# Attention and MLP kernel: batch 0 turned by float32 products on TensorE instead of DMA transposes, first matrix loaded in 4 KB rows

## Chip, core and metric

The kernel runs on one core of a Trainium2 chip. The metric is device time in microseconds (us) of one execution. The core has TensorE (PE, matrix products into PSUM), VectorE (DVE), ScalarE (ACT), GpSimd (POOL) and SyncE (SP), each with its own instruction queue that runs in order, and 16 DMA engines. SP's queue issues most transfers; ACT's queue issues the loads of the two weight matrices.

## The reference

Attention with a local window of 32 positions and 32 global tokens, over 8 batches and 8 heads, and behind it a two-layer MLP on the rows of the result:

```python
s_g = scale * q_g @ k_all.T;  out_g = sm(s_g) @ v_all          # 32 global rows
s_ll = where(abs(i - j) <= 32, scale * q_l @ k_l.T, -1e9)      # 512 local rows
s_l = concat([scale * q_l @ k_g.T, s_ll])
out_l = sm(s_l) @ concat([v_g, v_l])
x = concat([out_g, out_l]) as [8*544, 512]
h = x @ w_in                                                   # [512, 2048]
g = h * tanh(softplus(h))
return g @ w_out                                               # [2048, 512]
```

The two matrices arrive as 64-bit floats.

## The kernel before

**Numbers in two parts.** Products that must be exact run on pairs of float16 numbers: each operand is scaled by a power of two and split into a high part (rounded) and a low part (the remainder), and a product is three float16 products (high-high, high-low, low-high). This is done for probabilities (P to ph), for V (vraw to vf), for attention's result (x to xs), for both matrices (W) and for the MLP's middle (e to G).

**Attention.** A unit is (batch, pair of heads, quarter of 128 rows); there are 16 in a batch. `scores` makes two score tiles s (float32 products); `row_max` adds the mask and takes the row extreme into P on DVE; `expo` makes exponentials on ACT; `p_hi` and `p_lo` split P into ph; `p_turn` turns ph by a DMA transpose of 256 KB into pt, since the next product needs probabilities with the key along the partitions; `pv` multiplies pt with the moved parts of V (va, vc) into U. After two quarters (four, from batch 2 on) `x_norm`, `x_split` and `x_turn` divide, split and turn the result into xh and xl by two more DMA transposes. Global rows go the same way (g, gP, gph, gpt, gu).

**V.** `v_hi` and `v_lo` split, `v_move` places pieces by small SBUF to SBUF transfers.

**Weights.** Each matrix comes in 16 pieces of 512 KB (`w_load`, k below 16 is the first matrix w1). `w_bits` (L401) and `w_sum` (L408, L410) make 32-bit floats out of the 64-bit words, three DVE instructions a piece. `w_stat` sums squares on TensorE (tile ws, L421), `w_norm` (L428) reduces them to a scale once all 16 pieces are there, and only then `w_split` makes high and low parts of the eight column groups. The low part is either a DVE instruction (L471) or, for the groups in `BY_PE`, a product on TensorE: the scaled float32 original by a diagonal matrix dg (L465) minus the high part (L466) into a PSUM tile rest, copied by ACT or DVE. `BY_PE` holds the odd groups of both matrices.

**MLP.** The 4352 rows are 17 blocks of 256. `m1_mm` (L766, tile h) makes a step of the first layer, `mish` (L809) and `g_hi`, `g_lo` (L822) the activation and its parts, `m2_mm` (L834, tile o) the second layer, `store` the output.

**PSUM.** Ring h has two tiles (for the first layer, and for rest of the first matrix), o two, sc three for scores, u one.

**The order** is made by class `Plan` while the program is built: each task has an engine (or a choice of two), an estimated time, its dependencies and a priority; `order` simulates the engines by these estimates and emits each engine's list. Priorities follow `slot(u)`, which is called for each unit and the steps of blocks that `BLOCKS`, `PACE` and `LAGX` put beside it; `BOOST` is added to the MLP's tasks. Loads and conversions of the weights get slots from `LOAD1`, `CONV1`, `CONV2`, `FIRST1`, `FIRST2` and their steps. The estimate of a DMA transpose is `kib * 8` ns.

Of the kernel before, what the change touches and what calls it, by code (L numbers as in the profile page):

```python
# [49 lines left out]
class Plan:  # L50
# [10 lines left out]
    DEEP, SHARE, ISSUE = 3, 1.25, 450  # L61

    def __init__(self):
        self.tasks = []
# [24 lines left out]

    def add(self, eng, ns, fn, r=(), w=(), new=(), pri=0, rows=1.0, table=None):  # L90
# [41 lines left out]
        self.tasks.append((eng if isinstance(eng, list) else [(eng, ns)], fn, deps, after, new, n + pri + self.late if self.slot is None else -1e6 + self.slot * self.PER, rows, table))  # L132

    def order(self):
# [11 lines left out]
        moved, far = 0, []  # L146
# [40 lines left out]
        for _ in range(N):  # L187
            t, pri, e, n, ns = min(c for c in map(first, free) if c)
            start[n], on[n] = t, e
            if self.tasks[n][7] == "dma":  # L190
                far.append((max(t + self.DMA_IN, far[-1]) if far else t + self.DMA_IN) + ns * self.SHARE)
# [16 lines left out]
            if e == DMA:  # L208
                moved = max(moved, t) + ns
# [23 lines left out]
def attn_mish_kernel(ctx: ExitStack, tc: tile.TileContext, qt, kt, vm, vg, qg, w1, w2, consts_in, out, w64):  # L233
# [22 lines left out]
    def rings(pool, *table):  # L256
        for tag, bufs, shape, dt in table:
# [13 lines left out]
          ("wm", 2, [128, 1], F32), ("dg", 1, [128, 128], F32), ("pg", 1, [128, 2], F32), ("c", 3, [128, 3], F32),  # L271
# [102 lines left out]
    def words(k):  # L374
        return raw(k).rearrange("p (f w) -> p f w", w=2)

    def w_load(k):
        j, hf = HV[k]

        def go():  # L380
            n = 2 if w64 else 1
            dst = raw(k) if w64 else wf(k).bitcast(I32)
            if j < 8:
                nc.scalar.dma_start(dst.rearrange("p (c f) -> p c f", c=2),
                     w1[hf * 256:(hf + 1) * 256, j * 256 * n:(j + 1) * 256 * n].rearrange("(c p) f -> p c f", p=128))
# [6 lines left out]
        else:  # L392
            pl.add(ACT, dma(256), go, w=[wkey(j, hf)], table="dma")
# [3 lines left out]
    def w_bits(k):  # L397
        if not w64:
            return
        f, key = lambda: wf(k).bitcast(I32), wkey(*HV[k])  # L400
        pl.add(DVE, 360, lambda: V.tensor_scalar(f(), words(k)[:, :, 1], 3, 0x3FFFFFFF, ALU.logical_shift_left, ALU.bitwise_and),  # L401
               r=[rawkey(k)], w=[key])

    def w_sum(k):
        if not w64:
            return
        f, key = lambda: wf(k).bitcast(I32), wkey(*HV[k])
        pl.add(DVE, 610, lambda: V.scalar_tensor_tensor(f(), words(k)[:, :, 1], -0x40000000, f(), ALU.bitwise_and, ALU.bitwise_or),  # L408
               r=[rawkey(k)], w=[key])
        pl.add(DVE, 610, lambda: V.scalar_tensor_tensor(f(), words(k)[:, :, 0], 29, f(), ALU.logical_shift_right, ALU.bitwise_or),  # L410
               r=[rawkey(k)], w=[key])

    def w_stat(k):
# [3 lines left out]
        def go():  # L417
            u = wf(k).bitcast(BF16).rearrange("p (c two) -> p c two", two=2)
            for c in range(4):
                a = u[:, c * 128:(c + 1) * 128, 1]  # L420
                T.matmul(X["ws", w][:, :128], a, a, start=(k % 16 == 0 and c == 0), stop=(k % 16 == 15 and c == 3))  # L421
        pl.add(PE, mm(4, 131), go, r=[wkey(*HV[k])], w=[("ws", w)] if k % 16 else (),
# [51 lines left out]
    BY_PE = (1, 3, 5, 7, 9, 11, 13, 15)  # L474
# [632 lines left out]
```

## Time and profile before

| | us |
|---|---|
| runs | 1015.36, 1017.23, 1020.26; median 1017.23 |
| profiled execution, its own time | 1018.66 |
| its span, first to last instruction | 1016.9 |
| TensorE busy | 930.3 |
| ScalarE busy | 622.5 |
| VectorE busy | 566.0 |
| mean granted clock of TensorE | 0.991 |

Lines name L-number, engine, operation, and output tile<-input tiles. In rows of groups, busy time and mean ns of one stand after the first bar, idle time ahead of them and its releaser after the second. In rows of waits, the waiter stands left of the arrow; total us, times and longest follow. In rows of the timeline, start and length come first, and idle time before stands in brackets. In the lines of tenths a digit is the busy share in one of 40 equal slices. "SPq" and "ACTq" are the queues' issuing instructions. The product of two float32 operands shows as two MATMUL records, so "x2" at L465 is one product. PE's records overlap; from start to start is what one costs.

### The profile page before, as it was taken

Reading aid. Unit: us, or ns where it says so; the run is one execution under the profiler, and the core shown is the slowest. Engines: PE = TensorE matmul, PEld = TensorE weight load, DVE = VectorE, ACT = ScalarE, POOL = GpSimd, SP = SyncE. Lnnn points to the kernel's source line nnn. Section 1 sums busy time; section 2 is a strip of 40 time slices with the busy share of each in tenths; the row PEclk is TensorE's granted clock in tenths of the full one; section 3 lists DMA queues with packets and bytes.
Section 4 is the critical chain, followed back from the end, with each engine's and each line's share of the span. In section 5 each row is a group of like instructions: output and inputs, shape, how many; then the busy total and the mean of one; then the engine's idle time right before and its main releaser. Section 6 shows DMA issues by size and latency. Waiting matters only on the chain.

```text
span 1016.9 us, 20471 instructions
## 1 busy us (share of the span) xinstructions
PE 930.3 (91%) x7952; PEld 614.5 (60%) x7952; DVE 566.0 (56%) x1738; ACT 622.5 (61%) x1216; POOL 11.9 (1%) x22
## 2 busy tenths in 40 slices
PE   3245879999999899999999999999999999999996
PEld 2123555666656566666666666666666666666663
DVE  5468985657677655565556555655555554322221
ACT  2215586667667688689867986788688673211110
POOL 2000000000000000000000000000000000000000
PEclk9999989999999999999999999999999999999998
DMA  9996554747696975475446545644453432000000
GB/s 344 235 252 154 159 109 96 152 94 167 141 180 145 183 147 114 109 154 121 101 106 159 104 98 103 163 106 105 102 123 62 82 61 61 21 1 22 1 22 21
DMA packets 237946, 118.98 MB, mean 117 GB/s; under 512 B 202649, under 2 KB 216089, under 8 KB 236825
## 3 DMA queue, kind: packets, MB, share of 16 engines
q1 hardware_dynamic: 231192, 100.90, 46.1%
q10 hardware_dynamic: 6656, 16.78, 5.2%
q8 instruction: 62, 1.02, 0.4%
q14 instruction: 36, 0.29, 0.1%
HBM read 46.32 MB, written 8.91 MB: 54 GB/s over the span
## 4 chain that ended last, share of the span: by engine, by line
PE 78%; DMA 10%; DVE 6%; ACT 3%; SPq 2%; issue 1%; POOL 0%; ACTq 0%
PE o L834 32%; PE h L766 32%; PE s L579 5%; PE U L630 4%; DMA pt<-ph 3%; DMA vc<-vf 2%; PE g L668 2%; PE gu L722 1%; SPq L313 1%; DMA vraw<-in_vm 1%; DMA q<-in_qt 1%; DMA wraw<-in_w 1%; DVE W L410 1%; DVE W L408 1%; ACT P L594 1%
## 5 line engine op out<-in xcount | busy, mean ns | idle before, releaser
L834 PE MATMUL o<-W,G 128*128 128x512 f16 x1632 | 389.6, 380 | 1.8 <-DVE vmx L500 1.2
L766 PE MATMUL h<-xh,W 128*128 128x256 f16 x2048 | 378.6, 274 | 4.2 <-ACT e L809 4.2
L766 PEld LDWEIGHTS <-W 128*128 128x128 f16 x3264 | 309.0, 98 | 75.6 <-issue 15.9
L766 PE MATMUL h<-xl,W 128*128 128x256 f16 x1024 | 279.8, 273 | 0.0
L834 PEld LDWEIGHTS <-G 128*128 128x128 f16 x1632 | 156.7, 98 | 152.8 <-issue 5.7
L809 ACT ACTIVATE e<-h,c 128x512 f32<-128x512 f32 (+1 forms) x137 | 93.4, 684 | 150.8 <-PE h L766 144.0
L594 ACT ACTIVATE P<-P,nm 128x192 f32<-128x192 f32 (+1 forms) x256 | 118.0, 461 | 77.0 <-DVE nm L585 47.0
L326 DVE TENSOR_SCALAR G<-e,c 128x512 f16<-128x512 f32 (+1 forms) x136 | 65.5, 482 | 165.4 <-ACT e L809 164.8
L585 DVE CUSTOM_DVE_ANT_0 P<-s,consts 128x192 f32<-128x192 f32 (+1 forms) x256 | 91.3, 370 | 108.9 <-PE s L579 108.6
L613 DVE SCALAR_TENSOR_TENSOR ph<-P,ph 128x384 f16<-128x384 f32 (+1 forms) x128 | 75.0, 587 | 62.9 <-ACT ph L324 62.2
L809 ACT ACT_TABLE_LOAD x80 | 102.6, 1283 | 2.8 <-DVE G L822 1.3
L822 DVE SCALAR_TENSOR_TENSOR G<-e,c,G 128x512 f16<-128x512 f32 (+1 forms) x137 | 102.1, 746 | 2.5
L579 PE MATMUL s<-k,q 64*128 64x192 f32 (+1 forms) x512 | 88.1, 408 | 14.1 <-DMA q<-in_qt 11.5
L594 ACT ACT_TABLE_LOAD x73 | 93.7, 1283 | 1.3
L324 ACT ACTIVATE ph<-P 128x384 f16<-128x384 f32 (+1 forms) x127 | 68.9, 544 | 32.0 <-DMA pt<-ph 18.4
L630 PEld LDWEIGHTS <-pt 96*128 96x128 f16 (+1 forms) x1536 | 59.0, 99 | 46.9 <-DMA pt<-ph 24.5
L630 PE MATMUL U<-va,pt 128*128 128x64 f16 (+1 forms) x768 | 57.5, 196 | 23.9 <-DMA pt<-ph 20.2
L579 PEld LDWEIGHTS s<-k,q 64*128 64x128 f32 x512 | 43.4, 195 | 49.1 <-issue 31.3
L630 PE MATMUL U<-vc,pt 96*128 96x64 f16 x768 | 57.0, 195 | 0.0
L594 ACT ACTIVATION_READ_ACCUMULATOR P<-P,nm 128x1 f32 x256 | 47.8, 187 | 0.0
L324 ACT ACTIVATE xg<-gu,sv 64x32 f32<-64x32 f32 x64 | 18.0, 281 | 43.1 <-PE gu L722 42.7
L421 PE MATMUL ws<-W 128*128 128x128 bf16 x128 | 16.0, 262 | 29.8 <-DVE W L410 29.7
(94 smaller groups left out, 639.3 us busy)
## 6 DMA issues: line engine op xcount, KB each, us to landing
k<-in_kt SPq DMA_DIRECT2D x32, 320.0 KB, 3.4
wraw<-in_w ACTq DMA_DIRECT2D x17, 512.0 KB, 6.4
out<-ob SPq DMA_DIRECT2D x34, 256.0 KB, 2.3
q<-in_qt SPq DMA_DIRECT2D x32, 256.0 KB, 3.3
vraw<-in_vm SPq DMA_DIRECT2D x8, 1024.0 KB, 6.5
W<-in_w ACTq DMA_DIRECT2D x15, 512.0 KB, 5.8
vc<-vf SPq DMA_DIRECT2D x32, 128.0 KB, 2.4
va<-vf SPq DMA_DIRECT2D x32, 96.0 KB, 2.2
```

Source lines behind the costliest of these rows:

```text
L324: A.activation(out=dst, in_=src, func=AF.Copy, scale=c)
L326: V.tensor_scalar(dst, src, c, None, ALU.mult)
L579: T.matmul(X[s[h]][:, :w], X[q][r, t * 128:(t + 1) * 128], X[k][r, c0:c0 + w], start=True, stop=True)
L585: pl.add(DVE, 155 + 1.04 * w, lambda: V.tensor_tensor_reduce(out=X[P][:, h, :w], in0=X[s][:, :w], in1=mask[:, m0:m0 + w], scale=-SCALE, sc ...
L594: pl.add(ACT, 460, lambda: A.activation(out=X[P][:, h, :w], in_=X[P][:, h, :w], func=AF.Exp, bias=X[nm], scale=-1.0, accum_out=X[sums][:, ...
L613: pl.add(DVE, dve(n), lambda: V.scalar_tensor_tensor(p_part(X[ph], t, 1), p_src(X[P], t), PSC, p_part(X[ph], t, 0), ALU.mult, ALU.subtract ...
L630: T.matmul(X[u][:, t, h, :], X[pt][:k, p * 4 + h * 2 + c, :], X[vx][:k, t, vl, h * 64:(h + 1) * 64], start=(n == 0), stop=(n == 5))
L668: T.matmul(X[g][half * 64:half * 64 + 64, c0:c0 + n], X[q][:, hp, :], rhs, start=True, stop=True)
L766: T.matmul(X[h][:, f * TB:(f + 1) * TB], wh(i, wl)[:, off:off + 128], X[x][:, d, o:o + TB], start=(n == 0), stop=(n == 11))
L809: chain(blk, i, ACT, 705, lambda a, z: A.activation(out=X[e][:, a:z], in_=hv(blk, i)[:, a:z], func=AF.Mish, bias=0.0, scale=X[c][:, 0:1]), ...
L822: chain(blk, i, DVE, 668, lambda a, z: V.scalar_tensor_tensor(gp(1, blk, i)[:, a:z], X[e][:, a:z], X["c", blk][:, 2:3], gp(0, blk, i)[:, a ...
L834: T.matmul(X[o], gp(g, blk, i)[:, f, t * 128:(t + 1) * 128], wh(8 + i, wl)[:, f * 512:(f + 1) * 512], start=(i == 0 and n == 0), stop=(i = ...
```

## The change

For batch 0 (`TURNED = 1`) probabilities are no longer split and then turned by DMA. `p_cross` turns float32 P by four float32 products with the identity matrix into a PSUM tile PT (from ring h), and the split is made on the way out: high part by ACT or DVE, low part by DVE. `x_cross` does the same for x, into XT and straight to xh and xl. The low part of V in batch 0 is made by TensorE (tile VT, by a second diagonal matrix dv) and copied by ACT or DVE. Other batches keep the DMA transposes. The first matrix is loaded as pieces of 128 rows by 512 columns (4 KB rows of 64-bit words, where a row was 2 KB before), so a piece feeds two column groups. `BY_PE` becomes the eight groups of the first matrix; the low parts of the second are all DVE's. Splits are added to the plan where their slot comes up in the sequence of units. The planner's estimate for transposes is lowered, its model of two kinds of DMA traffic is changed to share, and a set of its constants has new values.

```diff
-    DEEP, SHARE, ISSUE = 3, 1.25, 450
+    DEEP, ISSUE = 3, 450
...
-                far.append((max(t + self.DMA_IN, far[-1]) if far else t + self.DMA_IN) + ns * self.SHARE)
+                s = max(t + self.DMA_IN, late)
+                both = min(ns, max(0, moved + self.DMA_IN - s))
+                moved += both
+                late = s + ns + both
+                far.append(late)
...
-          ("wm", 2, [128, 1], F32), ("dg", 1, [128, 128], F32), ("pg", 1, [128, 2], F32), ("c", 3, [128, 3], F32),
+          ("wm", 2, [128, 1], F32), ("dg", 2, [128, 128], F32), ("dv", 1, [128, 128], F32), ("pg", 1, [128, 2], F32), ("c", 3, [128, 3], F32),
...
+    kept("P", 3, [128, 480], F32, lambda x: x[:, 448:])
...
-            if j < 8:
-                nc.scalar.dma_start(dst.rearrange("p (c f) -> p c f", c=2),
-                     w1[hf * 256:(hf + 1) * 256, j * 256 * n:(j + 1) * 256 * n].rearrange("(c p) f -> p c f", p=128))
+            if k < 16:
+                c, f0 = k % 4, k // 4 * 512 * n
+                src = w1[c * 128:(c + 1) * 128, f0:f0 + 512 * n]
+                nc.scalar.dma_start(dst, src if w64 else src.rearrange("p (g f) -> p g f", g=2))
...
-    BY_PE = (1, 3, 5, 7, 9, 11, 13, 15)
+    BY_PE = range(8)
...
-        pl.add(DMA, kib * 8, lambda: nc.sync.dma_start_transpose(dst(), src()), r=r, w=w, new=new, rows=1300)
+        pl.add(DMA, kib * 6.8, lambda: nc.sync.dma_start_transpose(dst(), src()), r=r, w=w, new=new, rows=1300)
...
     def v_lo(b, hp):
         vf = ("vf", b, hp)
+        if b < TURNED:
+            d, VT = ("dv", b), ("VT", b, hp)
+            flat = lambda: X["vraw", b][:, hp].rearrange("p a c -> p (a c)")
+
+            def go():
+                T.matmul(X[VT], X[d], flat(), start=True, stop=False)
+                T.matmul(X[VT], minus, X[vf][:, :, 0, :], start=False, stop=True)
+            pl.add(PE, 780, go, r=[d, vf, ("vraw", b), "minus"], new=[("h", VT)], rows=0.5)
+            pl.add(EITHER, 0, lambda e: copy(e, X[vf][:, :, 1, :], X[VT].rearrange("p (a c) -> p a c", a=4)), r=[VT], w=[vf])
+            return
...
+    def p_cross(b, hp, t):
+
+        P, pt, PT = ("P", b, hp, t), ("pt", b, hp, t), ("PT", b, hp, t)
+        rows = 128 if t else 96
+
+        def go():
+            for h in range(2):
+                for c in range(2):
+                    c0, n = h * 224 + c * rows, h * 2 + c
+                    T.matmul(X[PT][:rows, n * 128:(n + 1) * 128], X[P][:, c0:c0 + rows], ident, start=True, stop=True)
+        pl.add(PE, 1000, go, r=[P, "consts"], new=[("h", PT)], rows=0.5)
+
+        def part(p):
+            return X[pt][:rows, p * 4:p * 4 + 4, :].rearrange("p n q -> p (n q)")
+        pl.add([(ACT, act(512)), (DVE, dve(512))], 0, lambda e: scaled(e, part(0), X[PT][:rows], PSC), r=[PT], new=[("pt", pt)])
+        pl.add(DVE, dve(512), lambda: V.scalar_tensor_tensor(part(1), X[PT][:rows], PSC, part(0), ALU.mult, ALU.subtract), r=[PT], w=[pt])
+
+    def x_cross(b, hp, t):
...
+        def go():
+            for i, u in enumerate(ts):
+                T.matmul(X[XT][:, i * 128:(i + 1) * 128], X[x][:, u].rearrange("p h d -> p (h d)"), ident, start=True, stop=True)
+        pl.add(PE, 250 * len(ts), go, r=[x, "consts"], new=[("h", XT)], rows=0.5)
...
         if bu:
-            p_hi(*bu)
-            p_lo(*bu)
-            p_turn(*bu)
+            if b < TURNED:
+                p_cross(*bu)
+            else:
+                p_hi(*bu)
+                p_lo(*bu)
+                p_turn(*bu)
...
-    BOOST = 74.486
+    BOOST = 125.042
...
-    FIRST1 = -0.412
-    STEP1 = 0.915
+    FIRST1 = 6.116
+    STEP1 = 0.588
```

What it moves, at three places. Names carry the build's running numbers. SP's queue near the program's start, behind the loads of batch 0 (pt_0_0 is the turned tile of pair 0, quarter 0; va and vc are the moved parts of V); before:

```order
L313 DMA qg_160<-in_qg 128x256
L482 DMA_TRANSPOSE pt_0_0_183<-ph_74 128x8x128
L482 DMA_TRANSPOSE pt_0_1_197<-ph_75 128x8x128
L313 DMA vgraw_225<-in_vg 128x256
L313 DMA va_0_234<-vf_0_219 64x256
L313 DMA vc_78<-vf_0_219 64x1024
```

and now:

```order
L322 DMA qg_219<-in_qg 128x256
L322 DMA vgraw_227<-in_vg 128x256
L322 DMA va_0_248<-vf_0_216 64x256
L322 DMA vc_84<-vf_0_216 64x1024
L322 DMA va_1_278<-vf_1_222 64x256
```

The transposes that stood ahead of V's moves are gone; up to batch 1 SP's list keeps only the four transposes of the global rows.

TensorE's list ahead of the first pv of batch 0; before:

```order
L421 MATMUL ws_155<-W 128x128
L579 MATMUL s_3_0_0_290<-k_3_135,q_3_137 128x192
L579 MATMUL s_3_0_1_291<-k_3_135,q_3_137 128x192
L630 LDWEIGHTS pt_0_0_183
L630 MATMUL U_0_0_304<-va_0_234,pt_0_0_183 128x64
```

and now, earlier in the list:

```order
L439 MATMUL ws_124<-W 128x128
L566 MATMUL VT_0_224<-vraw_109,dv_205 128x512
L567 LDWEIGHTS minus
L567 MATMUL VT_0_224<-vf_0_216,minus 128x512
L667 MATMUL PT_0_0_232<-consts,P_74 96x128 x4
L611 MATMUL s_1_1_0_243<-k_1_130,q_1_146 128x224
```

The products VT and PT now stand between the square sums ws and the scores s.

VectorE's list at the square-sum reduction of the second matrix (wd) and TensorE's at the first product of the second layer (o); before, VectorE:

```order
L326 TENSOR_SCALAR G_980<-e_1_999,c_678 128x512
L638 TENSOR_SCALAR rs_1_1_1103<-sums_1_1_730 128x4
L613 SCALAR_TENSOR_TENSOR ph_74<-P_2_2_1044,ph_74 128x2x224
L428 ISA wd_1109,wm_1108<-ws_706,consts 128x128
L428 ISA wm_1108 128x1
```

and TensorE:

```order
L630 MATMUL U_3_1_1515<-vc_81,pt_3_2_1457 128x64
L465 MATMUL rest_0_1531<-W,dg_1228 128x512
L466 LDWEIGHTS minus
L466 MATMUL rest_0_1531<-W,minus 128x512
L465 MATMUL rest_1_1548<-W,dg_1228 128x512
L466 LDWEIGHTS minus
L466 MATMUL rest_1_1548<-W,minus 128x512
L834 LDWEIGHTS G_980
L834 MATMUL o_0_1561<-W,G_980 128x512
```

Now VectorE has

```order
L427 SCALAR_TENSOR_TENSOR W<-wraw_1097,W 128x512
L335 TENSOR_SCALAR G_1188<-e_2_1166,c_741 128x512
L894 SCALAR_TENSOR_TENSOR G_1188<-e_2_1166,c_741,G_1188 128x512
L446 ISA wd_1204,wm_1203<-ws_657,consts 128x128
L446 ISA wm_1203 128x1
L689 TENSOR_TENSOR xl_414<-XT_0_1_1194,xh_403 128x256
```

and TensorE

```order
L838 MATMUL h_4_1252<-xl_414,W 128x256
L838 LDWEIGHTS W
L838 MATMUL h_4_1252<-xh_403,W 128x256
L906 LDWEIGHTS G_1066
L906 MATMUL o_0_1319<-W,G_1066 128x512
```

At the reduction, the same work of the first block stands ahead as before, within one step. The first o, which came behind h_7, three units' U and eight rest tiles of the second matrix, now comes behind h_4 with no rest tile of that matrix ahead of it.

More of the change, by code (lines that the diff above doesn't have):

```diff
@@ L131, in add @@
         after.discard(n)
-        self.tasks.append((eng if isinstance(eng, list) else [(eng, ns)], fn, deps, after, new, n + pri + self.late if self.slot is None else -1e6 + self.slot * self.PER, rows, table))
+        self.tasks.append((eng if isinstance(eng, list) else [(eng, ns)], fn, deps, after, new, n + pri + self.late if self.slot is None else self.base + self.slot * self.PER, rows, table))
     def order(self):
@@ L145, in order @@
         columns = {}
-        moved, far = 0, []
+        moved, far, late = 0, [], 0
         def tensor(t, ns, rows):
@@ L208, in order @@
             if e == DMA:
-                moved = max(moved, t) + ns
+                s = max(moved, t)
+                both = min(ns, max(0, late - s - self.DMA_IN))
+                late += both
+                moved = s + ns + both
                 free[e] = max(t + max(self.DMA_MIN, self.tasks[n][6]), moved - self.DMA_AHEAD)
@@ L392, in w_load @@
         else:
-            pl.add(ACT, dma(256), go, w=[wkey(j, hf)], table="dma")
+            pl.add(ACT, dma(256), go, w=wkeys(k), table="dma")
     def w_bits(k):
@@ L516, in b_split @@
     def b_split(b):
+        if b < TURNED:
+            d, s = ("dv", b), ("sv", b)
+            pl.add([(ACT, act(128)), (DVE, 220)], 0, lambda e: scaled(e, X[d], ident, X[s][:, 1:2]), r=["consts", s], new=[("dv", d)])
         sv, g, rg = ("sv", b), ("vgf", b), ("vgraw", b)
@@ L593, in expo @@
         first = t == ts[0] and h == 0
-        pl.add(ACT, 460, lambda: A.activation(out=X[P][:, h, :w], in_=X[P][:, h, :w], func=AF.Exp, bias=X[nm], scale=-1.0,
+        pl.add(ACT, 460, lambda: A.activation(out=half(P, h, w), in_=half(P, h, w), func=AF.Exp, bias=X[nm], scale=-1.0,
                                                               accum_out=X[sums][:, t, h:h + 1]),
@@ L618, in p_turn @@
         turn(256, lambda: X[pt], lambda: X[ph].rearrange("p a h k -> p (a h k)"), r=[ph], new=[("pt", pt)])
+    EITHER = [(ACT, act(512)), (DVE, dve(512))]
+    def p_cross(b, hp, t):
[12 more added lines that the diff above has]
+    def x_cross(b, hp, t):
+        g, ts = group(b, hp, t)
+        x, XT, n, c0 = ("x", *g), ("XT", *g), 128 * len(ts), ts[0] * 128
+        first = hp == 0 and ts[0] == 0
+        def go():
+            for i, u in enumerate(ts):
+                T.matmul(X[XT][:, i * 128:(i + 1) * 128], X[x][:, u].rearrange("p h d -> p (h d)"), ident, start=True, stop=True)
+        pl.add(PE, 250 * len(ts), go, r=[x, "consts"], new=[("h", XT)], rows=0.5)
+        hi, lo = ("xh", b), ("xl", b)
+        keys = [(hp, h) for h in range(2) if 2 * h in ts]
+        cut = lambda name: X[name][:, hp, c0:c0 + n]
+        pl.add([(ACT, act(n)), (DVE, dve(n))], 0, lambda e: copy(e, cut(hi), X[XT][:, :n]), r=[XT], w=[[hi, k] for k in keys],
+               new=[("xh", hi)] if first else ())
+        pl.add(DVE, dve(n), lambda: V.tensor_tensor(cut(lo), X[XT][:, :n], cut(hi), ALU.subtract), r=[XT] + [[hi, k] for k in keys],
+               w=[[lo, k] for k in keys], new=[("xl", lo)] if first else ())
     def pv(b, hp, t):
@@ L875, in unit @@
         return UNITS[u] if 0 <= u < NU else None
+    splits = []
     def slot(u):
+        while splits and splits[0][0] <= u:
+            pl.slot, j = splits.pop(0)
+            w_split(j)
+            pl.slot = None
         m, m2, md = (at(u - k) for k in (0, LAG2, LAG2 + 1))
@@ L1047, in attn_mish_kernel @@
     weights()
+    splits += [(FIRST1 + STEP1 * j, j) for j in range(8)] + [(FIRST2 + STEP2 * j, 8 + j) for j in range(8)]
+    splits.sort()
     for u in range(-1, max(S1[-1] + LAG2 + 2, NU + 2)):
```

96 lines of the change are left out of this document (53 added, 43 removed).

## The prediction

> **What bounds the kernel now.** First the page, for where TensorE is full.
>
> ```profile
> span 1016.9 us, 20471 instructions
> ...
> PE   3245879999999899999999999999999999999996
> ...
> DVE  5468985657677655565556555655555554322221
> ...
> DMA  9996554747696975475446545644453432000000
> ```
>
> A slice is 25.4 us. TensorE is full from the seventh on; DMA is full in the first three, VectorE nearly full in the fourth and fifth. So the time is a start in which TensorE starves, and a long stretch of nothing but TensorE work. The borders come from the timeline: the reductions of the square sums (L428) of the first and of the second matrix, and the first product of the second layer (o).
>
> ```profile
> 81.75 0.28 DVE L428 CUSTOM_DVE_ANT_0 wd<-ws,consts 128x128 f32<-128x128 f32 x1
> 127.99 0.29 DVE L428 CUSTOM_DVE_ANT_0 wd<-ws,consts 128x128 f32<-128x128 f32 x1
> 136.13 1.28 DVE L471 SCALAR_TENSOR_TENSOR W<-W,sw 128x1024 f16<-128x1024 f32 x1
> 162.51 0.81 PE L834 MATMUL o<-W,G 128*128 128x512 f16 x3 [0.40 <-ACT W L317]
> ```
>
> Busy time by stage (columns: stretch, its length, then PE, weight loads, DVE, ACT, POOL, granted clock, DMA share, GB/s):
>
> ```profile
> 0.00:81.75 81.75, 29.10 (x176) 17.74 (x176) 44.81 (x125) 18.99 (x55) 7.20 (x13) 1.00 1.02 277
> 81.75:128.30 46.55, 33.47 (x312) 22.55 (x312) 45.76 (x122) 29.47 (x53) 0.39 (x1) 1.00 0.56 143
> 128.30:162.51 34.21, 27.92 (x218) 17.85 (x215) 27.69 (x88) 28.46 (x58) 1.24 (x2) 0.90 0.47 97
> 162.51:1006.90 844.39, 839.83 (x7250) 556.32 (x7249) 447.01 (x1406) 545.50 (x1052) 3.07 (x6) 1.00 0.47 102
> 1006.90:1016.90 10.00, 0.00 (x0) 0.00 (x0) 0.75 (x1) 0.07 (x1) 0.00 (x0) 0.64 0.17 52
> ```
>
> Stage A (to 81.75) is DMA: its share is 1.02 and VectorE works only 44.8 of 81.75 us. Stage B (to 128) is VectorE, 98% busy. In stage C three engines are each about 0.82 busy. Stage D is TensorE; the last 10 us are the store. Why A is DMA's, from the chain of waits and the queues:
>
> ```profile
> PE ws L421 <- DVE W L410: 29.7, 18, 4.2
> PE U L630 <- DMA pt<-ph: 17.6, 5, 8.2
> DVE ph L613 <- ACT ph L324: 15.7, 4, 8.0
> ACT ph L324 <- DMA wraw<-in_w: 11.6, 1, 11.6
> 41.85 11.23 ACTq L384 DMA_DIRECT2D wraw<-in_w  x2
> 2.50:20.00 17.50, 5.98 (x20) 3.62 (x20) 8.06 (x25) 3.12 (x10) 5.23 (x8) 1.00 1.03 395
> 20.00:41.00 21.00, 8.17 (x49) 4.81 (x49) 13.30 (x42) 8.00 (x23) 0.00 (x0) 1.00 1.01 271
> 41.00:62.00 21.00, 6.22 (x52) 4.04 (x52) 11.35 (x26) 2.89 (x8) 0.00 (x0) 1.00 1.07 243
> 62.00:81.75 19.75, 8.73 (x56) 5.28 (x56) 12.04 (x33) 3.69 (x13) 0.00 (x0) 1.00 1.07 242
> ```
>
> Loads alone move 395 GB/s; once transposes and moves of V mix in, full engines move 243. ScalarE, which issues the weight loads, stands 11.23 us in one issue; its splits are late, and VectorE, in order, waits 15.7 us for them.
>
> **The parts and their costs.** The sum goes from the first o product: its time, plus the TensorE work left, plus gaps, plus the store. I added the instructions of each engine's order at the step of their kind in these rows (a row of two gives start to start).
>
> ```profile
> 71.71 0.75 DVE L401 TENSOR_SCALAR W<-wraw 128x512 int32<-128x512 int32 x2
> 72.38 1.29 DVE L408 SCALAR_TENSOR_TENSOR W<-wraw,W 128x512 int32<-128x512 int32 x2
> 73.58 1.29 DVE L410 SCALAR_TENSOR_TENSOR W<-wraw,W 128x512 int32<-128x512 int32 x2
> L822 DVE SCALAR_TENSOR_TENSOR G<-e,c,G 128x512 f16<-128x512 f32 x135 | 101.2, 749 | 2.4
> L585 DVE CUSTOM_DVE_ANT_0 P<-s,consts 128x224 f32<-128x224 f32 x128 | 48.0, 387 | 59.5 <-PE s L579 59.3
> 900.11 1.31 PE h L766 x12
> 901.42 1.29 PE o L834 x6
> 104.08 1.07 PE L465 MATMUL rest<-W,dg 128*128 128x512 f32 x2
> 104.98 0.38 PE L466 MATMUL rest<-W,minus 128*128 128x512 f16 x1
> 105.20 1.02 PE L465 MATMUL rest<-W,dg 128*128 128x512 f32 x2
> ```
>
> A conversion is 0.34+0.60+0.60 = 1.54 us, a low part of 512 columns 0.67, a row maximum about 0.37, a rest tile 1.12 (104.08 to 105.20). For the kernel before, this count gives VectorE 45.4 us to the first mark and 90.9 to the second, where the stages show 44.8 and 90.6: it may be used.
>
> *Stage A.* Removed up to the first mark: seven pt transposes of 256 KB and four x transposes of 64 KB from SP's queue, the waits of U for pt, and VectorE's wait for batch 1's V,
>
> ```profile
> 81.15 0.69 DVE L494 TENSOR_REDUCE vmx<-vraw 128x1 f32<-128x512 f32 x1 [3.40 <-DMA vraw<-in_vm]
> ...
> 5.46 0.92 DVE L401 TENSOR_SCALAR W<-wraw 128x512 int32<-128x512 int32 x1 [4.61 <-DMA wraw<-in_w]
> ```
>
> which (first row) stood ahead of the mark and now follows it: 4 us with certainty. What is behind SP's transposes, the moves of V and batch 1's loads, no longer waits for VectorE's splits. VectorE's list there is 39.7 us: 16 conversions 24.6, 15 row maxima 5.6, five low parts from PSUM 3.4 (priced as L822; a PSUM source may cost a little more, x<-U shows none), four V maxima 2.4, x and small ones 3.7. Starting at 5.5 (second row) it can't end before 45. The loads: 8.2 MB of first matrix, 4.2 of batch 0 and constants, 1.5 of V moves, 14 MB; at 395 GB/s they end near 39, at 243 near 61, and two conversions follow: 42 to 64. Between 45 and 64 I take 54: without transposes the rate is nearer the loads', but the small moves of V stay and ScalarE still issues loads among its work. The 4 KB rows I cost at nothing: they are the same bytes in the same queue, and what they gain is inside that rate. A P tile (three of them) is now held until TensorE has read it, not until the splits have; the row maximum three units later waits for it, and five units in 50 us leave that slack. The scaled identity dv and four copies of V lows go to ScalarE (19.0 busy of 81.75), the memsets of P to POOL (12 us busy in all): hidden. TensorE's list up to there is 19.4 us at full step; covered.
>
> *Stage B.* VectorE's list to the second mark is 46.6 us (before: 45.4): its 16 conversions stay, the four first-matrix lows it made leave, its six P lows come from PSUM as they came from SBUF. At 98% that is 47.5; at the 0.82 of stage C, where three engines were balanced, 57. TensorE has some 45 us in it (before 33), so I take 52. Second mark: 106.
>
> *To the first o.* Before, the first low part of the second matrix ended 9.4 us after the mark (136.13+1.28-127.99), and o came 25 us later because h products up to h_7 and eight rest tiles stood ahead of it. Now o follows h_4 at once and rest tiles of the second matrix are gone; its lows are VectorE's, eight at 1.2 us, four more than before, some 2.3 us apart in its list, near the 2.6 us that the o products of one low take. I take 9: first o at 115, bounds 102 and 130.
>
> *Added TensorE work.* A float32 transpose of two heads streams 4x128 columns like one L465 product: 0.85 us from the 1.07 row's overlap; with its four weight loads bare, up to twice that. 16 of these are 13.7 us (27 at most), eight x tiles 3.4, four V tiles 4.3. Eleven, five and all of them lie ahead of o, in stages with idle TensorE. Left after o: before 828 us by my count, where the stage lasted 844.4, so 16.5 of gaps; now 845, because five P and three x tiles (5.6), three pairs of h products (7.9) and 4 us of attention more stand behind it.
>
> *Stage D's order.* The order table's new numbers spread blocks and attention otherwise. TensorE's longest wait here is 2.4 us,
>
> ```profile
> PE U L630 <- DMA pt<-ph: 2.6, 2, 2.4
> ```
>
> so nothing is to be gained; the second matrix's splits may cost up to 8 us (the 36 us of work around them at 0.82 instead of full), I take 5. ScalarE and VectorE keep their cover elsewhere: 545 and 447 of 844.
>
> Sum: 54+52+9 = 115; +845+16.5+5+10 = 991.5 of span. The profiled execution took 1018.66 for 1016.9 of span, and 1.43 above the median of the runs, 1017.23; so **992 us**.
>
> **Rivals.** *TensorE stays slow* (ends slower). With gaps, products run at half step while the granted clock still reads 1.00:
>
> ```profile
> 88.62 2.06 PE L465 MATMUL rest<-W,dg 128*128 128x512 f32 x2
> 144.34 0.37 PE L766 MATMUL h<-xh,W 128*128 128x256 f16 x1 [4.25 <-ACT e L809]
> ...
> L766 PE MATMUL h<-xh,W 128*128 128x256 f16 x2048 | 378.6, 274 | 4.2 <-ACT e L809 4.2
> ```
>
> 2.06 us where the row at 104.08 has 1.07, and 0.37 for an h product after 4.25 us idle, whose kind has a mean of 0.27. TensorE's list to the first o is 69 us; at half step 138, from 6 on: o at 144 and 1021. It decides once o comes after 140. Against it: in stage B, with TensorE 72% busy, the steps were full at 104; half step in A alone is 39 us, still covered.
> The Trainium skill, "TensorE: Matmul & The Clock Gate", Part 1, states that half rate is the default and that about 3.4 us of sustained work releases it. The rows agree; by that rule a start of short bursts would stay at half rate throughout, and the sum would be this rival's 1021.
>
> *Two PSUM buffers* (no change). P, x, V, rest and h tiles all turn in the ring h of two: 45 tiles ahead of the first o. Before, eight rest tiles took from 88.62 to the row below plus its 0.38, 3.0 us each; 45 at that, from 8 on, put o at 143 and the end at 1020, which 0.5% can't tell from before. Against it: that pace was VectorE's, rest's own waits were 2.3 us.
>
> ```profile
> PE rest L466 <- ACT W L324: 2.3, 2, 1.6
> ...
> 112.25 0.38 PE L466 MATMUL rest<-W,minus 128*128 128x512 f16 x1
> ```
>
> *The transposes were cheap in DMA* (smaller gain). From 20 to 81.75 moved 15.6 MB, for which 395 GB/s need 39 us; of the other 22, eight transposes' worth of 256 KB could have 2.8 each, or V's small moves could have most. At 1 each the mark comes 8 us earlier, and the 4 us for V: 70, o at 131, 1008.
> The Trainium skill, "DMA: Bandwidth & Descriptors", Latency and other measured facts, gives 261 GB/s for a DMA transpose, an estimated 1 us for 256 KB; by that the sum is this rival's 1008. No run here times one alone. If the loads come no earlier at all, which would be the change not doing what it says, the first mark stays and 1018 comes out.
>
> *All at the lower bound* (more gain): o at 102, no new gaps: 973.5, so 974.
>
> **Numbers.** Forecast, 978 to 1003 (its terms' bounds add to 975 and 1011, which needs all at one end): 0.66. Cheap transposes, 1003 to 1012: 0.14. More gain: 0.07. No change (ring, late loads): 0.07. Slow TensorE: 0.06. A run can tell about 0.5%, 5 us. Faster 0.87, same 0.07, slower 0.06. Range 976 to 1012: it leaves out the no-change and slower cases and part of the largest gain.
>
> **What would show it.** First mark 45 to 64, second 96 to 118, first o 102 to 130; VectorE above 70% busy in A; no pt wait of U in A; TensorE waits of under 15 us after o. Wrong if TensorE's steps stay at 0.9 us in B, if h tiles wait on evictions for over 20 us, if the first mark comes after 70, or if the later stretch, which I left as it is, has gained waits on pt.

## The result and the profile after

The changed kernel took 990.08 us (median of four runs, 989.48 to 992.84), beside 1017.13 for the kernel before in the same runs: ratio 0.9736, 95% interval 0.9706 to 0.9766. It is 27 us faster; the forecast was 992. In two kernels below the profiled execution was slower than the others of the same kernel (spare8b: 1025.97 beside 1009.46 to 1010.90; turned2: 1139.81 at a mean granted clock of 0.842 beside 1029 to 1032), so ratios leave it out, and sizes read from its profile may be too large.

The page of the changed kernel, its span and the lines of tenths (a slice is 24.7 us):

```profile
span 987.5 us, 20674 instructions
...
PE   4789899999999999999999999999999999999995
...
DVE  6879777747777665755465556665555542322221
...
DMA  9875135766687975746383545654543430000000
```

TensorE is full from the sixth slice on, and nearly so from the third, where before it was at 4. DMA is full in the first slice and down to 1 tenth in the fifth.

The borders in its timeline (L446 is the reduction of a matrix's square sums, L428 before; L906 the first product of the second layer, L834 before):

```profile
53.41 0.29 DVE L446 CUSTOM_DVE_ANT_0 wd<-ws,consts 128x128 f32<-128x128 f32 x1
105.06 0.28 DVE L446 CUSTOM_DVE_ANT_0 wd<-ws,consts 128x128 f32<-128x128 f32 x1
115.22 2.85 PE L906 MATMUL o<-W,G 128*128 128x512 f16 x12
```

The forecast had 54, 106 and 115. Busy time by stretch (the columns as before; the first five rows are the stages A, B, C, D and the store, then the last part of stage A, then 20 to 60 us, then the kernel cut at 150 us):

```profile
0.00:53.41 53.41, 32.90 (x218) 21.78 (x219) 39.50 (x108) 17.35 (x46) 8.75 (x16) 0.90 0.91 316
53.41:105.34 51.93, 49.11 (x400) 32.46 (x400) 46.78 (x142) 34.13 (x69) 0.39 (x1) 0.93 0.55 178
105.34:115.22 9.88, 7.33 (x54) 5.24 (x53) 5.96 (x26) 8.80 (x21) 0.71 (x2) 1.00 0.06 18
115.22:977.50 862.28, 856.83 (x7458) 573.52 (x7455) 475.01 (x1461) 522.70 (x1052) 2.98 (x6) 1.00 0.48 101
977.50:987.50 10.00, 0.08 (x1) 0.00 (x0) 0.75 (x1) 0.16 (x1) 0.00 (x0) 0.68 0.17 52
...
41.00:53.40 12.40, 10.28 (x85) 7.86 (x86) 8.54 (x22) 3.04 (x8) 0.00 (x0) 0.72 0.95 305
...
20.00:60.00 40.00, 32.93 (x239) 22.37 (x239) 31.59 (x89) 18.83 (x52) 0.39 (x1) 0.87 0.91 299
...
0.00:150.00 150.00, 123.94 (x961) 82.42 (x962) 118.69 (x333) 88.85 (x184) 9.85 (x19) 0.94 0.61 200
150.00:977.50 827.50, 822.24 (x7165) 550.59 (x7163) 448.56 (x1400) 494.14 (x1003) 2.98 (x6) 1.00 0.48 101
```

Stage A is 28.3 us shorter, and VectorE is busy 74% of it (39.5 of 53.4) where it was 55%. Stage B is now full of TensorE (49.1 of 51.9) as well as of VectorE (46.8). The last row reads: behind 150 us TensorE works 822 of 827 us. The same cut of the kernel before:

```profile
0.00:150.00 150.00, 78.39 (x595) 50.41 (x596) 108.19 (x303) 66.22 (x141) 8.83 (x16) 0.98 0.81 211
150.00:1006.90 856.90, 851.94 (x7358) 564.04 (x7356) 457.07 (x1434) 556.20 (x1075) 3.07 (x6) 1.00 0.47 101
```

It too is full behind 150 us; it has done 595 recorded products by then instead of 961, and 30 us more are left (852 to 822). So the gain is made in the first 150 us, although TensorE has 172 product records more in all. What TensorE waits for now (first row stage A, the last two behind the first o):

```profile
PE ws L439 <- DVE W L427: 5.7, 5, 2.0
...
PE U L702 <- DMA pt<-ph: 3.0, 3, 1.4
PE gu L794 <- DMA gpt<-gph: 1.8, 1, 1.8
```

Over the whole span of the kernel before, the wait of ws for W was 29.7 us, and that of U for pt 17.6; 22.4 and 11.2 of these lay in stage A. In stage A of the changed kernel U waits for no pt any more. Behind the first o, waits sum to 5 us.

What one PT tile costs, in the timeline: eight records, start to start with the line behind it:

```profile
22.49 1.91 PE L667 MATMUL PT<-consts,P 128*96 128x128 f32 x8
24.34 1.12 PE L611 MATMUL s<-k,q 64*128 64x224 f32 x4
...
90.45 1.06 PE L667 MATMUL PT<-consts,P 128*128 128x128 f32 x8
91.35 0.39 PE L439 MATMUL ws<-W 128*128 128x128 bf16 x4
```

0.90 us in stage B, 1.85 in stage A, where TensorE's steps are slow.

### The profile page after: what moved, and what is told of

It is laid out like the page before. It is cut to its first block, busy times and chain, and to the rows that moved or that the text cites. A ratio compares the mean times of both kernels' runs of the same rounds, so it can differ in the third digit from the quotient of the medians.

```text
span 987.5 us, 20674 instructions
## 1 busy us (share of the span) xinstructions
PE 946.3 (96%) x8124; PEld 633.0 (64%) x8124; DVE 568.0 (58%) x1733; ACT 583.1 (59%) x1187; POOL 12.8 (1%) x25
## 3 DMA queue, kind: packets, MB, share of 16 engines
q10 hardware_dynamic: 4608, 16.78, 4.8%
## 4 chain that ended last, share of the span: by engine, by line
PE 81%; DMA 9%; DVE 5%; ACT 3%; SPq 2%; issue 1%; ACTq 0%; DVEq 0%
PE h L838 33%; PE o L906 32%; PE s L611 6%; PE U L702 4%; DMA vraw<-in_vm 4%; DMA pt<-ph 3%; PE g L740 2%; PE gu L794 2%; SPq L322 1%; PE rest L483 1%; DMA q<-in_qt 1%; DMA va<-vgf 1%; DVE vmx L512 1%; PE PT L667 1%; DVE W L489 0%
## 5 line engine op out<-in xcount | busy, mean ns | idle before, releaser
L906 PE MATMUL o<-W,G 128*128 128x512 f16 x1632 | 386.2, 379 | 0.0
L906 PEld LDWEIGHTS <-G 128*128 128x128 f16 x1632 | 155.1, 98 | 156.0 <-issue 8.5
L881 ACT ACTIVATE e<-h,c 128x512 f32<-128x512 f32 (+1 forms) x137 | 93.4, 683 | 165.1 <-PE h L838 157.2
L649 DVE SCALAR_TENSOR_TENSOR ph<-P,ph 128x384 f16<-128x384 f32 (+1 forms) x112 | 65.3, 586 | 71.6 <-ACT ph L333 71.1
L611 PE MATMUL s<-k,q 64*128 64x192 f32 (+1 forms) x512 | 84.2, 399 | 11.6 <-DMA q<-in_qt 11.1
L702 PEld LDWEIGHTS <-pt 96*128 96x128 f16 (+1 forms) x1536 | 59.6, 98 | 27.9 <-issue 10.7
L333 ACT ACTIVATE ph<-P 128x384 f16<-128x384 f32 (+1 forms) x110 | 59.7, 546 | 18.8 <-DMA pt<-ph 16.5
L611 PEld LDWEIGHTS s<-k,q 64*128 64x128 f32 x512 | 41.3, 190 | 41.8 <-issue 30.2
L333 ACT ACTIVATE ob<-o,c 128x512 f32<-128x512 f32 x33 | 22.6, 685 | 22.3 <-PE o L906 22.1
## 6 DMA issues: line engine op xcount, KB each, us to landing
vc<-vf SPq DMA_DIRECT2D x32, 128.0 KB, 2.3
```

The lines of the kernel that those rows point to most:

```text
L333: A.activation(out=dst, in_=src, func=AF.Copy, scale=c)
L611: T.matmul(X[s[h]][:, :w], X[q][r, t * 128:(t + 1) * 128], X[k][r, c0:c0 + w], start=True, stop=True)
L649: pl.add(DVE, dve(n), lambda: V.scalar_tensor_tensor(p_part(X[ph], t, 1), p_src(X[P], t), PSC, p_part(X[ph], t, 0), ALU.mult, ALU.subtract ...
L702: T.matmul(X[u][:, t, h, :], X[pt][:k, p * 4 + h * 2 + c, :], X[vx][:k, t, vl, h * 64:(h + 1) * 64], start=(n == 0), stop=(n == 5))
L881: chain(blk, i, ACT, 705, lambda a, z: A.activation(out=X[e][:, a:z], in_=hv(blk, i)[:, a:z], func=AF.Mish, bias=0.0, scale=X[c][:, 0:1]), ...
L906: T.matmul(X[o], gp(g, blk, i)[:, f, t * 128:(t + 1) * 128], wh(8 + i, wl)[:, f * 512:(f + 1) * 512], start=(i == 0 and n == 0), stop=(i = ...
```

## The experiments

**Theories.** Mine: turns by DMA held stage A back, about 2.8 us of full engines each; without them the first mark and all behind it come earlier. Rival 1: turns are cheap, about 1 us. Rival 2: the 4 KB rows carry part. Rival 3: which engine makes the low parts makes no difference. Rivals 4 to 7 stand in the expectations where they arise. "Theory now", 3' and 6' were formed after the first eight of the twelve experiments.

All runs; marks from the timelines, products from the cut at 150 us, "left" TensorE's busy time from there to 10 us before the end:

| kernel | us, median | ratio to before, 95% | first mark | second | first o | products by 150 | left |
|---|---|---|---|---|---|---|---|
| before | 1017 | 1 | 81.8 | 128.0 | 162.5 | 595 | 852 |
| changed | 990.1 | 0.9736 (0.9706–0.9766) | 53.4 | 105.1 | 115.2 | 961 | 822 |
| turned0 | 1006.3 | 0.9887 (0.9848–0.9926) | 70.9 | 119.7 | 139.7 | 696 | 839 |
| turn_only | 1024.5 | 1.0071 (1.0051–1.0091) | 55.4 | 74.3 | 133.6 | 692 | 855 |
| rows2k | 989.6 | 0.9744 (0.9697–0.9791) | 52.0 | 104.3 | 114.4 | 966 | 821 |
| lows_odd | 1019.3 | 1.0014 (0.999–1.0037) | 52.6 | 111.1 | 151.7 | 782 | 851 |
| spare8 | 1002.5 | 0.9851 (0.9786–0.9917) | 59.3 | 110.6 | 122.4 | 904 | 829 |
| pt_double | 1002.6 | 0.9852 (0.9812–0.9893) | 53.4 | 109.6 | 121.5 | 1008 | 835 |
| numbers_old | 992.2 | 0.9757 (0.9724–0.9789) | 53.2 | 106.4 | 116.6 | 938 | 826 |
| lows_only | 1015.6 | 0.9986 (0.9968–1.0004) | 82.6 | 122.8 | 135.9 | 669 | 840 |
| turn_lows | 1025.4 | 1.0085 (1.0059–1.011) | 55.7 | 74.3 | 133.5 | 692 | 855 |
| turn11 | 992.8 | 0.9772 (0.9752–0.9791) | 53.9 | 103.8 | 115.4 | 942 | 822 |

turned2 and spare8b are told below. Read down the last column: the kernel with more TensorE work left at 150 us is the slower one, but for some us (840 and 839 us, in lows_only and turned0, go with 1015.6 and 1006.3). In part this is arithmetic: behind 150 us TensorE idles only 4 to 11 us in every one of these kernels, so the work left is nearly the time left. What the column adds is where the difference arises: ahead of 150 us. Neither the first mark nor the first o alone ranks them.

### turned0: batch 0 without the new turning, everything else changed

```diff
-    TURNED = 1
+    TURNED = 0
```

> The changed kernel with TURNED = 0: batch 0 again splits, then turns by DMA; loads in 4 KB rows, low parts and the plan's numbers stay. Theory (the DMA turns are what held stage A back, some 2.8 us of full DMA engines each): the first mark goes back to 75 to 82 us, the first o to 138 to 150, the time to 1003 to 1016. Rival 1 (turns were cheap, about 1 us each, and the gain is the loads' rows or the plan's numbers): first mark 58 to 65, first o 120 to 130, time 990 to 999.

TURNED = 0 also gives V's low parts of batch 0 back to VectorE. 1006.3 us: 16 us of the 27 go with the turning, within the theory's range. The first mark, at 70.9, lies between the two forecasts. So 17.5 us of the 28.3 at this mark are the turning's; the other 11 come without it. What VectorE waits for up to the mark (rows of its waits):

```profile
DVE ph L649 <- ACT ph L333: 8.7, 5, 4.7
DVE W L418 <- DMA wraw<-in_w: 4.6, 1, 4.6
DVE W L418 <- DMA W<-in_w: 3.3, 1, 3.3
```

In stage A, VectorE stands 8.7 us for ScalarE's share of splits and about 8 for weight loads. Up to the mark it has 50.9 us of work, 11.4 more than in the changed kernel (in stage B 39.8, 7 less): three conversions, the four low parts of V and five row maxima more. It has 20 us of idle time, 6 more. So two thirds of the 17.5 us, seen from VectorE, are its longer list. The idle time, however, is DMA's in the main. Its waits for weight loads were 5.9 us in the changed kernel, so they grew by 2; and 6.5 of the 8.7 us are for two splits that ScalarE began late, behind the issue of a weight load, after idle time that the profile puts down to transposes of x:

```profile
53.29 0.52 ACT L333 ACTIVATE ph<-P 128x384 f16<-128x384 f32 x1 [8.07 <-DMA xl<-xs]
67.11 0.52 ACT L333 ACTIVATE ph<-P 128x384 f16<-128x384 f32 x1 [5.13 <-DMA xh<-xs]
```

DMA's share up to the mark is 1.02 here and 0.91 in the changed kernel. How much of the mark's delay the list alone would have made was not tried.

### spare8 and spare8b: eight transposes put back that nobody reads

The spare transposes of 256 KB turn a tile of zeros; they sit on SP's queue among V's moves (spare8), or four behind pair 1's and four behind pair 2's last move (spare8b). Every other instruction keeps its order.

```diff
+    def spare(u):
+        y = X[("xh", "xl")[u % 2], "spare"][...]
+        nc.sync.dma_start_transpose(y, blank.rearrange("p a h k -> p (a h k)"))
...
+        AT = {(0, 0): 1, (0, 1): 1, (0, 5): 1, (1, 0): 1, (1, 1): 1, (1, 5): 1, (2, 0): 1, (2, 5): 1}    # spare8
+        AT = {(1, 7): 4, (2, 7): 4}                                                                      # spare8b
+            # behind move i of pair hp: AT[hp, i] transposes
```

> The changed kernel with eight more DMA transposes of 256 KB, which turn a tile of zeros into a spare tile that nobody reads, put between V's moves of pairs 0 to 2 on SP's queue (23 to 45 us); the order of every other instruction is as in the changed kernel. Theory (2.8 us of all DMA engines each): the first mark 53.4 + 15 to 22, so 68 to 76, and the time 1000 to 1010. Rival 1 (1 us each): first mark 57 to 62, time 992 to 997. Rival 4 (DMA no longer ends stage A): first mark within 2 us of 53.4.

First mark 59.3, so 5.9 us later: rival 1's range, not mine. The median time, 1002.5, lies in my range, but its spread (994.6 to 1008.0) reaches into rival 1's as well, so it decides less. Its window from 20 to 60 us, to be read beside the changed kernel's row above:

```profile
20.00:60.00 40.00, 25.29 (x192) 17.52 (x193) 27.15 (x75) 14.00 (x38) 0.27 (x1) 0.86 1.13 296
```

VectorE's longest wait up to 60 us, and the wait of TensorE behind it (1.9 us in the changed kernel):

```profile
DVE x L731 <- PE U L721: 6.1, 1, 6.1
...
PE U L721 <- DMA va<-vgf: 7.5, 2, 6.1
```

DMA's share of these 40 us rises from 0.91 to 1.13, which is 8.8 us. That is too little for a price, because less of the weights moved in this window, 7.87 MB instead of 9.07. The page has the sums over the span: for each queue packets, MB, and the time that these took as a share of the span of all 16 engines. The first row is SP's queue with all transposes, the second ACT's with the weight loads alone; two rows each for the changed kernel, spare8 and turned0:

```profile
q1 hardware_dynamic: 209688, 95.65, 44.2%
q10 hardware_dynamic: 4608, 16.78, 4.8%
...
q1 hardware_dynamic: 218136, 97.75, 45.0%
q10 hardware_dynamic: 4608, 16.78, 4.8%
...
q1 hardware_dynamic: 231192, 100.90, 46.8%
q10 hardware_dynamic: 4608, 16.78, 5.8%
```

In spare8 the first queue takes 448.6 us of all engines (45.0% of 996.8) instead of 436.5: 12 us for eight, 1.5 us each, and the weight loads take no more than in the changed kernel. In turned0, whose turning of batch 0 moves 5.25 MB more, twenty times 256 KB, it takes 33.6 us more, 1.7 us for 256 KB; and there the same 16.78 MB of weights take 58 us instead of 47. With that, 256 KB cost about 2.2 us.

The mark's delay in spare8 is about the size of one wait: U for a move of V (va) that now lies behind transposes on its queue, and VectorE, in order, for U. The Trainium skill, "DMA: Bandwidth & Descriptors", Latency and other measured facts, gives 261 GB/s for a DMA transpose with a non-contiguous middle dimension and some 350 to 400 for a contiguous one, an estimated 0.7 to 1.0 us for 256 KB; this run's 1.5 is more than either.

From that I took it that only the queue's order mattered:

> The changed kernel with the same eight spare DMA transposes of 256 KB, now behind the last move of V of pair 1 (four, at 36 us) and of pair 2 (four, at 48 us) on SP's queue; the order of all else unchanged. Theory now (a transpose takes next to nothing from the weight loads; the 6 us it cost the mark was one wait of U for a move of V that stood behind transposes): first mark 53 to 56 and time 989 to 995. Rival 1 (they take DMA time from the loads, 0.74 us or more each): first mark 58 to 62 again.

Theory and rival were both wrong: 1010.8 us, and in the profile a first mark at 72.1. SP's issues in its timeline:

```profile
37.26 1.37 SPq L580 DMA_TRANSPOSE xh_spare<-ph  x1
38.68 2.83 SPq L580 DMA_TRANSPOSE xl_spare<-ph  x1
41.55 1.72 SPq L580 DMA_TRANSPOSE xh_spare<-ph  x1
43.31 8.34 SPq L580 DMA_TRANSPOSE xl_spare<-ph  x1
51.75 0.54 SPq L323 DMA_DIRECT2D va<-vf  x1
```

TensorE's longest wait:

```profile
PE U L721 <- DMA va<-vgf: 15.2, 2, 14.4
```

The window in which the first four are under way:

```profile
40.00:52.00 12.00, 4.60 (x57) 3.86 (x57) 7.65 (x17) 2.51 (x6) 0.00 (x0) 0.77 1.15 162
```

Issued in a row, they fill the DMA engines (share 1.15) while only 162 GB/s move, the fourth blocks SP for 8.34 us, and a move of V behind them is 14.4 us late for U. So what a transpose costs is no constant. Spread, it was 1.5 us of DMA time. Bunched, it was 3.2: the queue takes 461.9 us in this profile (45.1% of 1024.2), 25.4 more than in the changed kernel, and the weight loads take 11 us more. To that comes what stands behind it on its queue. In the kernel before, two at 74.52 us took SP 6.53 us.

### turn_only, lows_only and turn_lows: one part at a time, from the kernel before

```diff
+    TURNED = 1                      # turn_only, turn_lows: p_cross, x_cross, v_lo and kept P as in the change
-    BY_PE = (1, 3, 5, 7, 9, 11, 13, 15)
+    BY_PE = range(8)                # lows_only, turn_lows
```

> The kernel before with the float32 turning of batch 0 (P, x, low part of V) alone: old 2 KB rows, old low parts, old numbers of the plan. Theory: the first mark comes at 54 to 62 us as in the changed kernel, but the old order still puts all steps up to h_7 and eight more rest tiles ahead of the first o, so that this comes 25 to 34 us behind the second mark, at 130 to 142; with less work left behind it the time is 992 to 1002. Rival 1 (the gain is the rows or the numbers): first mark above 70, time above 1006.

1024.5 us, slower than before by 0.5 to 0.9%. The theory was right on the marks and wrong on the time, the rival the other way round: the first mark came as early as forecast, at 55.4, the first o inside its range, at 133.6, and yet the time grew. The stage up to the first mark, and its timeline in VectorE at two places:

```profile
0.00:55.40 55.40, 15.10 (x80) 8.77 (x80) 43.15 (x100) 7.65 (x19) 7.37 (x16) 1.00 0.97 359
```

```profile
33.13 0.42 DVE L402 TENSOR_SCALAR W<-wraw 128x512 int32<-128x512 int32 x1
33.46 0.68 DVE L409 SCALAR_TENSOR_TENSOR W<-W 128x512 int32<-128x512 int32 x1
...
53.14 1.28 DVE L411 SCALAR_TENSOR_TENSOR W<-wraw,W 128x512 int32<-128x512 int32 x2
```

Between 24 and 55 us VectorE makes nothing but conversions (L402, L409, L411). With the old numbers and the old place of the weights in the plan, it converts the second matrix on end as well (second mark at 74), while attention waits: 80 TensorE products up to the first mark, where the changed kernel has 218 at the same time. The marks came early because attention was put off, and TensorE had 855 us left at 150.

> The kernel before with BY_PE = the first matrix's eight groups, and nothing else. Together with the kernel that has the turning alone and the one that has all but the new low parts. Theory now (what counts is TensorE work done early, and the low parts of the first matrix on TensorE let the h products start, which needs rows of x as well): with the turns still by DMA the first mark stays at 79 to 84 and the time falls little, 1008 to 1016. Rival 3' (the low parts carry the gain by themselves): 1000 or less.

1015.6, not told apart from before, as the theory had it (ratio 0.9968 to 1.0004). The first o comes 27 us earlier, at 135.9, and is worth little, since other work stands behind it instead.

> The kernel before with the turning and the new low parts, but old rows, old plan model and old numbers. Theory now (turning and low parts need each other): 990 to 1000, with 900 or more TensorE products done by 150 us. Rival 6' (the order that the plan's numbers and model give is needed as well, as the turning alone suggests): 1008 or more, and under 750 products done by 150 us.

1025.4: rival 6' held. The low parts add nothing to turn_only; its marks and its 692 products are the same. So the order in which loads, conversions and splits are placed, which this kernel lacks, is the part without which the others don't pay. The reverse, that order without the turning and without the new low parts, was not run.

### numbers_old and rows2k: parts that carry nothing much

```diff
-    BLK2 = 25.461
+    BLK2 = 29.824
...
-    BOOST = 125.042
+    BOOST = 74.486                  # numbers_old; BLK3, LAGX, PACE and the estimate of a transpose too
```

> The changed kernel with the old values of BLK2, BLK3, LAGX, PACE and BOOST and the old estimate of a transpose. Theory (the spread of blocks and attention over the full stretch is worth little, the start sets the time): first mark 53 to 56, time 988 to 996. Rival 6 (the numbers carry part of the gain): 1000 or more, with first mark unchanged and the loss behind the first o.

992.2, as the theory had it. So of the plan's numbers those for the blocks carry some 2 us. With turn_lows and rows2k this leaves the slots of loads, conversions and splits, and the planner's model of DMA traffic, for the order's part; these two weren't parted.

```diff
...
-                src = w1[c * 128:(c + 1) * 128, f0:f0 + 512 * n]
...
+                     w1[hf * 256:(hf + 1) * 256, j * 256 * n:(j + 1) * 256 * n].rearrange("(c p) f -> p c f", p=128))
```

> The changed kernel with the first matrix again loaded in the old pieces of 2 KB rows. Theory (rows cost nothing, same bytes in the same queue): first mark within 3 us of 53.4, time within 3 us of 990. Rival 2 (the rows carry part of the gain): first mark 60 or later, time 995 or more.

989.6 and a first mark at 52.0: the 4 KB rows are worth nothing here; rival 2 falls.

### lows_odd: the low parts on the old engines

```diff
-    BY_PE = range(8)
+    BY_PE = (1, 3, 5, 7, 9, 11, 13, 15)
```

> The changed kernel with BY_PE = odd groups of both matrices, as before. Theory: first mark unchanged (53 to 55); stage B gets four more low parts of VectorE (2.4 to 5 us in all later second mark), and TensorE gets 8 rest tiles of the second matrix (9 us of work) and loses 8 of the first in a stage where it has room: time 992 to 999. Rival 3 (it does not matter which engine makes them): 989 to 991.5.

1019.3: the whole gain is gone, far beyond the theory's 992 to 999. The first mark is where it was (52.6). Its stage B, from there to the second mark, and stage C up to the first o:

```profile
52.90:111.40 58.50, 43.64 (x378) 30.91 (x374) 52.20 (x154) 31.79 (x70) 0.55 (x1) 0.85 0.50 161
111.40:151.65 40.25, 29.57 (x194) 17.95 (x195) 20.61 (x58) 29.41 (x50) 0.93 (x2) 0.86 0.25 66
```

With four more low parts VectorE has 52.2 us of work in stage B (46.8 in the changed kernel); the stage is 6.6 us longer, and TensorE idles 15 us in it. Then eight rest tiles of the second matrix stand ahead of the first o, in the ring h of two tiles that PT and h use too. One place in TensorE's timeline:

```profile
121.03 0.27 PE L838 MATMUL h<-xh,W 128*128 128x256 f16 x1
124.74 2.07 PE L667 MATMUL PT<-consts,P 128*128 128x128 f32 x8 [3.44 <-ACT e L881]
```

A PT tile waits 3.44 us for a buffer that ScalarE's activation (L881) still reads, and then runs at half step, 2.07 us. Stage C takes 40 us instead of 10; TensorE idles 10.7 of them. That stage C has these waits is shown; which of them alone would bring it back was not tried.

### pt_double: the price of the products

```diff
-            for h in range(2):
+            for h in (0, 1, 0, 1):
```

> The changed kernel with each of the 16 PT tiles made twice (all its products issued again into the same tile); order otherwise as it was. 16 times 0.85 to 0.9 us more TensorE work. Theory (eleven of them lie where TensorE waits, five behind the first o): marks and first o within 3 us, time 4 to 8 us more, 994 to 998. Rival 5 (the turning is on the path in the start as well, by TensorE or by the ring of two PSUM tiles): all of it shows, 14 us or more, 1004 and up.

1002.6, 12.5 us more than the changed kernel: nearer rival 5 than my 4 to 8. Sixteen extra tiles, so 0.78 us each. By stage:

```profile
0.00:53.39 53.39, 33.59 (x258) 23.82 (x259) 39.27 (x107) 17.36 (x46) 8.76 (x16) 0.97 0.88 311
53.39:109.87 56.48, 53.07 (x448) 37.42 (x448) 47.54 (x142) 34.20 (x69) 0.38 (x1) 0.97 0.54 169
109.87:121.48 11.61, 8.87 (x54) 6.05 (x52) 7.27 (x31) 10.22 (x23) 0.71 (x2) 0.85 0.17 41
121.48:992.30 870.82, 863.06 (x7498) 577.75 (x7495) 474.36 (x1457) 521.45 (x1051) 2.98 (x6) 1.00 0.47 99
```

In stage A the 40 added records (five tiles) cost nothing. In stage B 48 (six tiles) lengthen it by 4.6 us, which is about what they take (six at 0.9 are 5.4). Stage C is 1.7 us longer with no tile added in it. Behind the first o five more tiles stand beside 8.5 us, more than their 4.5; where the rest of these two comes from was not traced. Stage B, which I had called VectorE's, is TensorE's as much.

### turn11 and turned2: fewer or more tiles turned by TensorE

```diff
-            if b < TURNED:
+            if u < 11:                   # turn11
...
-    TURNED = 1
+    TURNED = 2                           # turned2
```

> The changed kernel, but only the first 11 units of batch 0 are turned by TensorE; the last five of its 16, most of which lie behind the first o, are split and turned by DMA as in the other batches. Theory (behind the first o each product counts in full, and the DMA turn is hidden there): 5 times 0.9 us less TensorE work, 984 to 988. Rival (the DMA turn's latency or the extra splits come back as waits of U and as late h products): 989 to 996.

992.8 (990.5 to 995.3), the rival's range. TensorE has 40 records less, but 942 products by 150 us instead of 961, and as much time left, 822: what it is spared it loses in the start, and TensorE idles 7.6 us behind 150 us, 2.3 more. The two largest sums of its waits behind 100 us:

```profile
PE U L702 <- DMA pt<-ph: 3.8, 6, 1.6
PE gu L794 <- DMA gpt<-gph: 2.3, 4, 1.1
```

> The changed kernel with TURNED = 2: batch 1 turned by TensorE too. Theory (in the full stretch each product adds to the sum): batch 1's 16 PT, 8 x halves and 4 V tiles are 21 us of TensorE work, most behind the first o: 1003 to 1012. Rival 7 (batch 1's turns by DMA still hold the start back): first o earlier by 5 or more and time 980 to 990.

Ratio 1.0135 (1.0092 to 1.0178); the time is about 1031 us. That is slower, as the theory said, but by some 40 us, about twice its amount. By the expectation's count 21 of them are the products added; where the others come from stays open. The first o is at 118.5 in the profile, not earlier, so rival 7 falls. No version that was run beats the changed kernel: rows2k equals it.

## Why the prediction was right, and where it was not

- **Stage A, 54: measured 53.4.** VectorE's list was counted at 39.7 and is 39.5. The cause that I gave is only a part of it. With the turns back in DMA the mark moved by 17.5 of 28.3 us, and 11.4 of these stand beside a longer list of VectorE, which the prediction used for a bound alone. The price of 2.8 us of DMA for a turn was too high: 1.5 where they are spread, about 2.2 in turned0 with what the weight loads lose. The bounds that the list and the loads gave, 45 and 64, held; the choice of 54 between them was not worked out, so that it came within 0.6 us is luck.
- **Cheap transposes, the rival at 1008.** Its price of 1 us was too low, and its conclusion was wrong, a mark at 70: it, too, counted little but DMA's time as what the turning saves.
- **4 KB rows at nothing:** shown by rows2k.
- **Stage B, 52: measured 51.9**, VectorE 46.78 where 46.6 was counted. The prediction counted some 45 us of TensorE work in it and took the added products for hidden. That was wrong: it is 49.1 us busy, and pt_double lengthens the stage by the products put into it.
- **To the first o, 9: measured 9.9.**
- **A PT tile at 0.85 us:** 0.90 in the trace, 0.78 by doubling. The prediction called eleven of sixteen hidden; it is five.
- **Stage D, 866.5 (845+16.5+5): measured 862.3.** The 17 us of added work are borne out: TensorE is busy 856.8 us there, before 839.8. What the sum called 16.5 us of gaps was in the main work that the count had left out: the kernel before idles 4.6 us in stage D (844.39-839.83). The 5 us of new gaps, for the second matrix's splits among TensorE's work, did not come; TensorE's idle time behind the first o is 5.5 us in all (862.28-856.83). This is the term that was mis-sized, by about 4 us, and it makes the difference in span (987.5 for 991.5).
- **The order.** The prediction said that nothing was to be gained in stage D's order, and numbers_old bears that out to 2 us. In the start, however, the gain needs three parts at once: without the turning it is 1006 us, without the new low parts 1019, without the new order 1025. The sum did not fail on it because its lists were counted from the order as built, low parts and all: the 25 us that it took off stage C need the low parts, and lows_odd, without them, has 40 us there. The text gave stage A's gain to the turning alone.
- **Slow TensorE.** Its steps were at half in parts of stage A (1.85 us for a PT tile, 0.90 later), and this was covered there, as the prediction had it. The Trainium skill, "TensorE: Matmul & The Clock Gate", Part 1, has half rate as the default until some 3.4 us of sustained work; these two steps agree, and the start did not stay at half rate.
- **Two PSUM buffers.** Not in the changed kernel, whose longest wait on an eviction up to the first o is 2.2 us. It does show in lows_odd, in the wait of 3.4 us shown.

## What to carry to other kernels

Where one engine is full to the end, ask of each edit how much of that engine's work will be done by a fixed early time; a milestone that comes earlier says little if other work was put off for it. A part of a change tried alone can lose what the whole wins, since the order was made for the whole. A DMA transpose cost most here by what waited behind it on its queue, so spread them and keep small urgent moves ahead.

## What the runs showed of the hardware

- Eight DMA transposes of 256 KB spread over some 29 us took 1.5 us of the 16 engines each; four in a row held the issuing queue for 8.34 us at the last, with 162 GB/s moved at a share of 1.15.
- The 16.78 MB of weight loads took 47 us of the 16 engines in the changed kernel and in spare8, and 58 us in turned0, where batch 0's DMA turns run beside them.
- In the changed kernel's stage A the granted clock reads 0.72 from 41 to 53 us, though TensorE is busy 10.3 of 12.4 us; in the kernel before it reads 1.00 in stages A and B, although a product at 88.62 us took 2.06 us there, half its later pace. So the granted clock of a stretch does not tell the step; the time from start to start does.
